# A transformer block with recurrent memory, forward and backward on one core: block-diagonal products in the backward loop and new priorities for its planner

## The chip, the cores and the metric

The kernel runs on one core of one Trainium2 chip. The metric is the device time of one execution in microseconds. The core has five engines with instruction queues of their own: PE (TensorE, matmuls; its weight loads are listed apart as PEld), DVE (VectorE), ACT (ScalarE), POOL (GpSimd) and SP (SyncE, which here only issues DMAs). SBUF is the memory on the chip in which engines read and write; PSUM takes the results of matmuls, here in eight banks.

## The reference

The output is the input x plus a memory-augmented attention of xn plus a squared-ReLU MLP of xn, where xn is the layer norm of x. All gradients (of x, the initial memory, four attention weights, two MLP weights and two biases) are outputs too. x has 2048 rows of 512; there are 32 heads of 128. What matters here is the attention, a recurrence over 64 segments:

```python
for s in range(n_seg):                       # 64 segments of 32 rows, M = 8
    xs = x[:, s * seg_len:(s + 1) * seg_len, :].copy()
    h = jnp.concatenate([mem, xs], axis=1)   # 8 memory rows, 32 tokens
    q = jnp.einsum('btd,dhe->bhte', h, Wq)
    k = jnp.einsum('btd,dhe->bhte', h, Wk)
    v = jnp.einsum('btd,dhe->bhte', h, Wv)
    scores = jnp.einsum('bhqe,bhke->bhqk', q, k) * scale
    scores = jnp.where(mask[None, None], scores, -1000000000.0)
    p = _softmax(scores, axis=-1)
    o = jnp.einsum('bhqk,bhke->bhqe', p, v)
    o = jnp.einsum('bhte,hed->btd', o, Wo)
    mem = o[:, :M, :].copy()                 # memory of the next segment
    outs.append(o[:, M:, :])
```

The backward pass walks the segments from the last to the first: the gradient of a segment's memory rows is an input of the segment before it, so the 64 segments form one chain.

## The kernel before, in words

The program has three stages: the forward pass, the backward loop over the segments, and the weight gradients as large products, which read back from memory (HBM) what the loop stored. Only the backward loop is changed.

In the loop the 32 heads lie as 8 groups (index i, NI = 8) of 4 (index j, JQ = 4); head (i, j) has its rows on the 32 partitions of quadrant j. Four segments make a block (SPB = 4, 16 blocks). The rows of a segment are split in two sets: the rows of the segment's chain ("A"), and the leading tokens ("L"), the first 8 tokens of each segment, 32 rows a block, which don't wait for the recurrence and are done for a whole block at once.

For each block `l_pre` does the leading tokens' part: it loads their V, K, Q and P, computes gL (the incoming gradient times Wo), dP (ps_dPL), the softmax's backward on DVE (btL, dSL), its transpose dSTLL, and dQ (ps_dqL, into dLN). `l_post` computes their gradients of x (ps_dRL) from what was stored. For each segment `load` fetches its operands and lets POOL spread some of them into block-diagonal tiles: BDP, BDL, BPK, BLK, BSLK, BDSL. `chain` is the recurrence itself:

- ps_gO: the segment's gradient rows times Wo; ps_gOT: their transposes, copied to SBUF as gOT by DVE or ACT
- ps_dP: from gOT and V; then `smax_bwd` on DVE, four steps on btA and brA, whose last writes dS into the tile named maskA
- after dS, on DVE: the copy of its memory columns to dSp, and two transposes, dSTA and dSTL, which lie in the tile named PB; POOL spreads dS's memory columns into BSK
- dV (part 2, `blocks`), dK (part 1, `mixed`) and dQ (part 0, `diag`): products into PSUM (ps_d), copied to dN by ACT or DVE, transposed to dT by DVE and multiplied by the weights (ps_dRA, 32 matmuls each, all three into one bank)
- ps_dL: the gradients of dK and dV for the leading tokens (`keys_part`)
- R_A: the sum, copied out of PSUM in two halves; ps_gm picks its memory rows, and DVE writes them over the memory rows of the gradient of the segment before (tile gT, a part of PA). With that copy (PA<-ps_gm) a segment ends, and the next one's ps_gO may begin.

`blk_out` transposes the block's gradient rows back (ps_gN), copies them to the tile gNat and stores them in S_GOA for the weight gradients.

A product of 32x32 pieces, one for each head, can be made in two ways. `diag` gives each head a matmul of 32 rows on 32 columns at its own place in the array, 16 for four groups. `blocks` needs the four heads of a group side by side in one tile with zeros elsewhere (block-diagonal) and makes one matmul of 128 on 128 for them.

The order of the instructions is not the order of the source. Each call of `plan.add` records an operation with its cost on each engine that may do it; `_Plan.run` then places them one by one. An operation's rank is the length of the work that hangs on it plus a number of its own from the table BIAS, and three numbers in PAR say how the rule weighs waiting. Each engine executes its queue in the order found.

## Time and profile before

| | |
|---|---|
| time, median of 3 runs | 2801.01 us (2796.82 to 2802.35) |
| span of the profiled execution, first to last instruction | 2798.3 us |
| busy in the span | PE 95%, PEld 55%, DVE 47%, ACT 35%, POOL 29% |
| granted TensorE clock, mean | 0.995 |
| instructions | 125071 |

The page gives the profiled execution as its span; no other time of it is listed. A page's busy PE includes what a pipelined matmul waits inside the array, so PE at 95% is not PE at its peak. Rows of the profile name a line, an engine, an operation and output<-inputs by tile; a line can be that of a helper that many operations share, so the tile names tell them apart. "issue" is time for which the profile names no wait.

### The profile page before, as it was taken

The page shows a single profiled execution, that of the slowest core. Times are in us where ns is not written, and L with a number is a line of the kernel's source. Part 1 is how long each engine was busy: PE and PEld are TensorE (multiplying, and loading weights), DVE is VectorE, ACT ScalarE, POOL GpSimd, SP SyncE. Part 2 cuts the span into 40 slices and gives each one's busy share as a digit, 9 for nine tenths or more (in the row PEclk, how much of TensorE's full clock was granted, in tenths as well). Part 3 has the DMA queues.
Part 4 walks back from the last instruction along what each step waited for, and adds up shares of the span by engine and source line. Part 5 has one row for each costly group of instructions (what it writes and reads, how often), then busy time and mean ns, then how long its engine had stood idle before and what let it go on. Part 6 is the DMA issues. An engine that isn't in the chain of part 4 may idle for free.

```text
span 2798.3 us, 125071 instructions
## 1 busy us (share of the span) xinstructions
PE 2664.6 (95%) x54888; PEld 1538.5 (55%) x55072; DVE 1327.3 (47%) x3327; ACT 985.8 (35%) x2012; POOL 824.8 (29%) x2431
## 2 busy tenths in 40 slices
PE   8998999999999999999999999999999899999999
PEld 6664555555555555575555555555555444444444
DVE  5544455555455555565455455555455402232322
ACT  4333444444444444364444444444444300000000
POOL 1111111111111111145555555555555301112210
PEclk9999999999999999999999999999999999999999
DMA  6657656555557566647777676777766698788861
GB/s 211 202 172 205 180 160 175 164 166 163 156 169 186 169 185 175 177 118 178 187 181 187 179 189 179 189 192 190 188 182 177 201 344 273 232 255 270 257 185 42
DMA packets 499792, 530.91 MB, mean 190 GB/s; under 512 B 223845, under 2 KB 325398, under 8 KB 497070
## 3 DMA queue, kind: packets, MB, share of 16 engines
q1 hardware_dynamic: 480254, 463.06, 59.9%
q0 software_dynamic: 15056, 53.56, 5.6%
q8 instruction: 430, 7.05, 1.1%
q10 hardware_dynamic: 3936, 6.29, 0.7%
q14 instruction: 116, 0.95, 0.1%
HBM read 249.77 MB, written 237.52 MB: 174 GB/s over the span
## 4 chain that ended last, share of the span: by engine, by line
PE 45%; DVE 4%; issue 3%; DMA 3%; ACT 1%; POOL 1%; SPq 0%; DVEq 0%; ACTq 0%; POOLq 0%
PE ps_gw L1690 14%; PE ps_dRA L1370 8%; PE ps_gw L1694 5%; PE ps_gO L538 3%; PE ps_dRL L1370 3%; PE ps_d L624 2%; DMA dLN<-S_GNL 2%; PE ps_d L573 1%; PE ps_d L599 1%; PE ps_gOT L429 1%; PE ps_d L588 1%; PE ps_gm L1524 1%; PE ps_gL L538 1%; PE ps_dL L1481 1%; PE ps_dP L1468 1%
## 5 line engine op out<-in xcount | busy, mean ns | idle before, releaser
L1370 PE MATMUL ps_dRA<-WA,dT 128*32 128x512 bf16 x6144 | 377.0, 381 | 5.3 <-issue 2.5
L1690 PE MATMUL ps_gw<-WA,WB 128*128 128x512 bf16 x1505 | 330.6, 379 | 1.6
L1690 PEld LDWEIGHTS <-WB 128*128 128x128 bf16 x1896 | 185.4, 98 | 225.0 <-issue 1.7
L538 PEld LDWEIGHTS <-PA 128*32 128x32 bf16 x8192 | 195.4, 96 | 192.3 <-DVE PA L1190 22.3
L435 ACT CAST dN<-ps_d 128x512 bf16<-128x512 f32 x372 | 207.4, 590 | 184.7 <-PE ps_d L599 112.3
L1370 PEld LDWEIGHTS <-dT 128*32 128x32 bf16 x6144 | 151.8, 96 | 154.2 <-DVE dT L517 17.3
L433 DVE CAST gwo<-ps_gw 128x512 bf16<-128x512 f32 x64 | 40.0, 685 | 399.9 <-PE ps_gw L1690 268.5
L435 ACT CAST gwo<-ps_gw 128x512 bf16<-128x512 f32 x64 | 33.1, 598 | 510.2 <-PE ps_gw L1690 357.3
L517 DVE STREAM_TRANSPOSE dT<-dN 128x256 f32<-128x256 f32 x384 | 165.4, 437 | 72.1 <-ACT dN L435 66.5
L1020 POOL TENSOR_TENSOR P<-P,rsA 128x320 bf16<-128x320 bf16 x64 | 46.2, 722 | 458.8 <-DVE rsA L1015 244.1
L624 PEld LDWEIGHTS <-PB 32*32 32x32 bf16 x8192 | 119.8, 92 | 76.4 <-DVE PB L1168 23.9
L1701 POOL DMA_DIRECT2D out_dram<-gwo x96 | 71.6, 753 | 293.9 <-ACT gwo L435 265.1
L538 PE MATMUL ps_q<-WA,PA 128*32 128x512 bf16 x2048 | 145.2, 382 | 5.5 <-DVE PA L1190 3.7
L1039 PE MATMUL ps_RA<-WB,OT 128*32 128x256 bf16 x4096 | 129.0, 277 | 17.7 <-DVE OT L517 13.6
L538 PE MATMUL ps_k<-WA,PA 128*32 128x512 bf16 x2048 | 144.9, 381 | 0.3 <-DVE PA L1190 0.3
L435 ACT CAST kN<-ps_k 128x512 bf16<-128x512 f32 x125 | 73.4, 587 | 194.1 <-PE ps_k L538 172.2
L538 PE MATMUL ps_v<-WA,PA 128*32 128x512 bf16 x2048 | 140.7, 379 | 0.0
L1039 PEld LDWEIGHTS <-OT 128*32 128x32 bf16 x4096 | 103.9, 98 | 46.2 <-DVE OT L517 32.0
L538 PE MATMUL ps_gO<-WB,PA 128*32 128x512 bf16 x2048 | 126.4, 380 | 1.0 <-DVE PA L1528 1.0
L611 POOL COPY BDL<-bPLL 32x64 bf16<-32x64 bf16 x256 | 60.4, 236 | 218.4 <-PE ps_d L573 210.4
L433 DVE CAST qN<-ps_q 128x512 bf16<-128x512 f32 x62 | 42.9, 692 | 171.5 <-PE ps_q L538 169.5
L1254 PE MATMUL ps_dw<-sx,anT 128*128 128x512 bf16 x339 | 108.2, 384 | 6.6 <-DMA sx<-S_XN 2.8
(315 smaller groups left out, 5300.8 us busy)
## 6 DMA issues: line engine op xcount, KB each, us to landing
S_GN<-dN SPq DMA_DIRECT2D x192, 256.0 KB
WA<-S_GN SPq DMA_DIRECT2D x150, 256.0 KB
S_Q<-qN SPq DMA_DIRECT2D x64, 256.0 KB
S_K<-kN SPq DMA_DIRECT2D x64, 256.0 KB
S_V<-vN SPq DMA_DIRECT2D x64, 256.0 KB
S_ON<-oN SPq DMA_DIRECT2D x64, 256.0 KB
bqN<-S_Q SPq DMA_DIRECT2D x64, 256.0 KB
bkN<-S_K SPq DMA_DIRECT2D x64, 256.0 KB
```

The lines of the kernel that those rows point to most:

```text
L433: nc.vector.tensor_copy(out, in_)
L435: nc.scalar.copy(out, in_)
L517: self.plan.add({"DVE": 0.445}, lambda e, half=half: nc.vector.transpose(words(dst, half).rearrange("p (i c r) -> p i c r", i=4, c=2), src ...
L538: nc.tensor.matmul(bk()[32 * j:32 * (j + 1), :], lhsT=win(dc), rhs=Wt(dc, c0), start=(dc == 0), stop=(dc == DC - 1), tile_position=(0, 32 ...
L611: f(q_(dst, j)[:, :, j, 0:c], q_(src_f(), j))
L624: nc.tensor.matmul(bk()[32 * j:32 * j + m, k * P:(k + 1) * P], lhsT=lf(j, i), rhs=rf(j, i), start=(k == 0 and x == 0), stop=(x == n - 1), ...
L1039: nc.tensor.matmul(bk()[32 * c:32 * (c + 1), :], lhsT=sg.rows(OTt, i, j), rhs=Wo[:, JQ * i + j, dh * DH:(dh + 1) * DH], start=(i == 0 and ...
L1254: nc.tensor.matmul(bks[x]()[:], lhsT=anT[x][:, c, :], rhs=sx[z][:], start=(c == 0), stop=(c == TC - 1))
L1370: nc.tensor.matmul(bk()[32 * j:32 * (j + 1), :], lhsT=sg.rows(XT, i, j), rhs=wtf(t, i, j), start=(first and i == 0), stop=(last and i == N ...
L1690: nc.tensor.matmul(bks[n](), lhsT=HNc[:, rc, dc * P:(dc + 1) * P], rhs=gns[y][:, hf * 512:(hf + 1) * 512], start=(y == 0), stop=(y == NRC ...
L1694: nc.tensor.matmul(bks[n](), lhsT=gns[y][:, k * P:(k + 1) * P], rhs=GOc[:, rc, :], start=(y == 0), stop=(y == NRC - 1))
L1701: nc.gpsimd.dma_start(outWs[t][dc * P:(dc + 1) * P, 4 * hf:4 * hf + 4, j, :], wt[:].rearrange("p (i e) -> p i e", i=4))
```

## The change

All that changes lies in the backward loop.

- dK's chain term: `mixed` can now take block-diagonal terms (`full=True`). dS is spread into a new tile BDS, and 8 matmuls of 128x128 take the place of 32 of 32x32. The two banks of this product have a kind of their own ("x") instead of sharing three with the others.
- The leading tokens' dQ: the two terms' transposed dS is copied into a new block-diagonal tile BDQ, half a block's groups and one term at a time, and 16 matmuls of 128x128 take the place of 64 small ones.
- The leading tokens' dP: V of the memory rows and V of the leading tokens lie in one tile (V3), so one matmul of 64 columns takes the place of two of 32.
- `blk_out`: only the memory rows are transposed and copied out of the chip's memory, 32 rows of 128 columns in four matmuls side by side; the other rows, which the loop doesn't change, go from the gradient's input to S_GOA directly. There are 8 DMAs a block instead of 4.
- PAR's third entry and the whole table BIAS_2 are new, and with them the order.

```diff
-PAR = ((0.3, 0.3, 0.0), (0.61, 7.94, 4.04), (0.09, 2.05, 17.32))
+PAR = ((0.3, 0.3, 0.0), (0.61, 7.94, 4.04), (0.1, 0.72, 43.97))
...
-        34.6, 126.2, 225, -84.9, 411.2, 93.4, -139.6, 40.8, -2.7, -1, 50.3, -26.5, 101.4, 73.6, 181.6, -48.1,
+        15.7, 24.2, 97.5, -336.6, -23, -15.5, -22.7, 0, 6.5, -136.5, -220.1, -237.4, -153.9, -142.5, -8.8,
...
-        def mixed(self, nm, pre, terms, rkeys, dst, prio, lift=0.0):
+        def mixed(self, nm, pre, terms, rkeys, dst, prio, lift=0.0, full=False, inter=False, kind=None):
 
-            bks = [self.bank("d", [P, 512], F32, "ps_" + nm) for _ in range(2)]
+            bks = [self.bank("x", [P, 512], F32, "ps_" + nm) for _ in range(2)]
...
                         for x, (lf, rf) in enumerate(terms):
+                            if full:
+                                nc.tensor.matmul(bk()[:, k * P:(k + 1) * P], lhsT=lf(i), rhs=rf(i),
+                                                 start=False, stop=(x == len(terms) - 1), skip_group_check=True)
+                                continue
                             for j in range(JQ):
...
-        VTL = [tl("VTL%d" % x, TR) for x in range(2)]
...
-        LT0, LT1 = (tl("LT%d" % x, TR) for x in range(2))
+        LT0, V3 = tl("LT0", TR), tl("V3", [P, 3, NI, JQ, RA])
+        VTL, LT1 = [V3[:, 1], V3[:, 0]], V3[:, 2]
+        V2 = [V3[:, 1:3], V3[:, 0:3:2]]
...
+        BDS = tl("BDS", TR)
...
+        BDQ = tl("BDQ", [P, NI // 2, JQ, RL])
+        nc.gpsimd.memset(BDQ[:], 0.0)
...
                 for i in range(NI):
-                    for c, VX in enumerate((VTL[p], VTM)):
-                        for j in range(JQ):
-                            nc.tensor.matmul(q_(bk(), j)[:, i, 32 * c:32 * c + 32], lhsT=LT0[:, i, j, :],
-                                             rhs=VX[:, i, j, :], start=(i == 0 and c == 0), stop=True,
-                                             tile_position=(0, 32 * j), skip_group_check=True)
-            A(pe(0.45, "w", 64), dp, both("LT0") + both("LT1") + [("VTL", p)], [bk, "btL"])
+                    for j in range(JQ):
+                        nc.tensor.matmul(q_(bk(), j)[:, i, :], lhsT=LT0[:, i, j, :], rhs=V2[p][:, :, i, j, :],
+                                         start=(i == 0), stop=True, tile_position=(0, 32 * j), skip_group_check=True)
+            A(pe(0.3, "w", 32), dp, both("LT0") + both("LT1") + [("VTL", p)], [bk, "btL"])
...
-            sg.diag("f", "dqL", [
-                (lambda j, i: q_(dSTLL, j)[:, i, 0, :], lambda j, i: q_(kLN[p], j)[:, i, :], 32),
-                (lambda j, i: q_(dSTLL, j)[:, i, 1, :], lambda j, i: q_(KM, j)[:, i, :], 32),
-            ], lambda h: ["dSTLL", K("kLN")] + both("LT1"), ("dLN", dLN), 1)
+            for h in range(2):
+                bq = sg.bank("f", [P, 512], F32, "ps_dqL")
+                for c, X in enumerate((kLN[p], KM)):
+                    for j in range(JQ):
+                        def cp(e, c=c, j=j, h=h):
+                            f = {"DVE": nc.vector.tensor_copy, "POOL": nc.gpsimd.tensor_copy}[e]
+                            f(q_(BDQ, j)[:, :, j, :], q_(dSTLL, j)[:, 4 * h:4 * h + 4, c, :])
+                        A({"DVE": 0.13, "POOL": 0.28}, cp, ["dSTLL"], [("BDQ", j)], 1)
+
+                    def mm(e, h=h, bq=bq, c=c, X=X):
+                        for k in range(4):
+                            nc.tensor.matmul(bq()[:, k * P:(k + 1) * P], lhsT=bd(BDQ, k), rhs=X[:, 4 * h + k, :],
+                                             start=(k == 0 and c == 0), stop=(c == 1), skip_group_check=True)
...
             sg.spread(BSK, "BSK", lambda: dS[:, :, 0:M], ["dS"], M, 0, {"POOL": 0.235})
+            sg.spread(BDS, "BDS", lambda: dS[:, :, M:KA], ["dS"], RA, 0, {"DVE": 0.17, "POOL": 0.41})
             part(1, lambda dst: sg.mixed(
                 "d1", [(lambda i: bd(BDSL, i), lambda i: qLN[p][:, i, :])],
-                [(lambda j, i: q_(dS, j)[:, i, M:KA], lambda j, i: q_(qN, j)[:, i, :])],
-                (lambda h: [K("qLN")] + bk4("BDSL"), lambda h: ["qN", "dS"]), dst, 0), False, False)
+                [(lambda i: bd(BDS, i), lambda i: qN[:, i, :])],
+                (lambda h: [K("qLN")] + bk4("BDSL"), lambda h: ["qN"] + bk4("BDS")), dst, 0, full=True), False, False)
...
-            bk = sg.bank("f", [P, D], BF16, "ps_gN")
+            A({"POOL": 0.3}, lambda e: nc.gpsimd.tensor_copy(
+                gNat[:, 0:P].rearrange("p (c v k) -> p c v k", c=DC, k=M), gT[p].rearrange("p c (v r) -> p c v r", r=RA)[:, :, :, 0:M]),
+              [("gT", p)] + [("gm", p, v) for v in range(SPB)], ["gNat"])
+            bk = sg.bank("f", [P, P], F32, "ps_gN")
...
-                    transpose_to(bk()[:, dc * P:(dc + 1) * P], gT[p][:, dc, :])
-            A(pe(0.222, "f", 4), tr, [("gT", p)] + [("gm", p, v) for v in range(SPB)], [bk, "gNat"])
-            sg.evict(lambda: gNat, bk, lambda: bk()[:], ["gNat"], 1, EV_B)
+                    nc.tensor.matmul(bk()[32 * dc:32 * (dc + 1), :], lhsT=gNat[:, 32 * dc:32 * (dc + 1)], rhs=ident[:],
+                                     start=True, stop=True, tile_position=(0, 32 * dc), skip_group_check=True)
...
+            for dc in range(DC):
+                sg.dma(lambda dc=dc: S_GOA[b * P:(b + 1) * P, dc * P:(dc + 1) * P].rearrange("(r v) d -> v r d", v=SPB)[:, 0:M],
+                       lambda dc=dc: gNat[32 * dc:32 * (dc + 1), P:2 * P], ["gNat2"], [])
             for v in range(SPB):
-                sg.dma(lambda v=v: S_GOA[b * P:(b + 1) * P, :].rearrange("(r v) d -> v r d", v=SPB)[v],
-                       lambda v=v: gNat[RA * v:RA * (v + 1)], ["gNat"], [])
+                sg.dma(lambda v=v: S_GOA[b * P:(b + 1) * P].rearrange("(r v) d -> v r d", v=SPB)[v, M:],
+                       lambda v=v: gflat[b * P + RA * v + M:b * P + RA * (v + 1)], [], [])
```

In the order that the planner finds, 254 of the 256 copies into BDS stand on DVE and 2 on POOL; of the 256 into BDQ 222 stand on DVE and 34 on POOL. Three places show what moves.

DVE, from dS to the transposes of dK and dQ, in the segment v = 2 of a block. The tile maskA is dS, PB holds its two transposes; dT_31380 and dT_31379 are those of dK and dQ before, dT_31378 that of dK after. Before:

```order
L1359 SCALAR_TENSOR_TENSOR maskA<-btA,bP_31372 128x320
L1500 COPY dSp_31345<-maskA 128x8x8
L1502 STREAM_TRANSPOSE PB<-dSp_31345 128x256
L1501 STREAM_TRANSPOSE PB<-maskA 128x256
L517 STREAM_TRANSPOSE dT_31380<-dN_31377 128x256 x2
L517 STREAM_TRANSPOSE dT_31379<-dN_31376 128x256 x2
```

After:

```order
L1376 SCALAR_TENSOR_TENSOR maskA<-btA,bP_31370 128x320
L624 COPY BDS<-maskA 32x8x32 x4
L1526 COPY dSp_31345<-maskA 128x8x8
L1527 STREAM_TRANSPOSE PB<-maskA 128x256
L1528 STREAM_TRANSPOSE PB<-dSp_31345 128x256
L518 STREAM_TRANSPOSE dT_31378<-dN_31375 128x256 x2
```

The four copies into BDS come first behind dS, and the copy and the transposes that dQ needs come behind them.

TensorE, from dP to dQ's product, in a segment that has the leading tokens' ps_dRL beside it; the first matmul of each group is shown. dT_31381 (before) and dT_31379 (after) belong to dV. The products with maskA or BDS are dK's chain term, with BDSL its leading term for the next segment, with PB dQ's. Before:

```order
L1468 MATMUL ps_dP<-bVT,gOT 32x40
...
L1370 MATMUL ps_dRL<-WA,LT_31360 32x512
...
L1370 MATMUL ps_dRA<-WA,dT_31381 32x512
...
L599 MATMUL ps_d_48441<-bqN,maskA 32x128
...
L1370 MATMUL ps_dRA<-WA,dT_31381 32x512
...
L624 MATMUL ps_d_49005<-bkN,PB 32x128
```

After:

```order
L1494 MATMUL ps_dP<-bVT,gOT 32x40
...
L1387 MATMUL ps_dRL<-WA,LT_31358 32x512
...
L1387 MATMUL ps_dRA<-WA,dT_31379 32x512
...
L607 MATMUL ps_d_46965<-bqN,BDS 128x128
...
L589 MATMUL ps_d_47427<-bqLN_31349,BDSL 128x128
...
L637 MATMUL ps_d_47433<-bkN,PB 32x128
```

Before, half of dV's 32 ps_dRA matmuls stand between dK's and dQ's products; after, all of them stand ahead of dK's, and only the four matmuls with BDSL stand between.

DVE, in the segment in which the leading tokens' softmax ends. Before:

```order
L1528 CAST PA<-ps_gm 128x4x8
L433 COPY LT_31360<-ps_gLT 128x512
L1354 TENSOR_TENSOR btL<-ps_dPL,bPLL_31357 128x512
L1356 TENSOR_REDUCE brL<-btL 128x8
L1357 TENSOR_TENSOR btL<-ps_dPL,brL 128x512
L517 STREAM_TRANSPOSE dT_31381<-dN_31378 128x256
L1359 SCALAR_TENSOR_TENSOR dSL_31359<-btL,bPLL_31357 128x512
```

After:

```order
L1555 CAST PA<-ps_gm 128x4x8
L1374 TENSOR_TENSOR btL<-ps_dPL,brL 128x512
L1376 SCALAR_TENSOR_TENSOR dSL_31357<-btL,bPLL_31355 128x512
L1425 STREAM_TRANSPOSE dSTLL<-dSL_31357 128x512
L1433 COPY BDQ<-dSTLL 32x4x32 x4
L434 COPY gOT<-ps_gOT 128x512
L1433 COPY BDQ<-dSTLL 32x4x32 x3
L434 COPY gOT<-ps_gOT 128x512
```

The softmax's first two steps moved into the segment before, and seven copies into BDQ stand ahead of the two gOT copies, for which ps_dP waits.

More of the change, by code (lines that the diff above doesn't have):

```diff
@@ L601, in mm @@
                                                  skip_group_check=True)
-                self.plan.add(pe(0.222 * len(terms), "d", 16 * len(terms)), mm, rkeys[1](half), [bk], prio)
+                cost = pe(0.22 * len(terms), "f", 4 * len(terms)) if full else pe(0.222 * len(terms), "d", 16 * len(terms))
+                self.plan.add(cost, mm, rkeys[1](half), [bk], prio)
                 self.evict(lambda half=half: dst[1][:, 4 * half:4 * half + 4, :].rearrange("p i e -> p (i e)"),
@@ L1331 @@
         BDP, BDL, BDSL = (tl(n, TR) for n in ("BDP", "BDL", "BDSL"))
-        for t_ in (BDP, BDL, BDSL):
+        BDS = tl("BDS", TR)
+        for t_ in (BDP, BDL, BDSL, BDS):
             nc.gpsimd.memset(t_[:], 0.0)
+        BDQ = tl("BDQ", [P, NI // 2, JQ, RL])
+        nc.gpsimd.memset(BDQ[:], 0.0)
         BPK, BLK, BSK, BSLK = (tl(n, [P, NI, JQ, M]) for n in ("BPK", "BLK", "BSK", "BSLK"))
```

45 lines of the change are left out of this document (28 added, 17 removed), and 27 rows, old and new, of the table BIAS_2.

## The prediction

> **What bounds the kernel now.** I read the page first, for the share of each engine, then the stretch of the backward loop alone, then the loop's own clock.
>
> ```profile
> span 2798.3 us, 125071 instructions
> PE 2664.6 (95%) x54888; PEld 1538.5 (55%) x55072; DVE 1327.3 (47%) x3327; ACT 985.8 (35%) x2012; POOL 824.8 (29%) x2431
> ...
> 1260.00:2209.00 949.00, 911.21 (x25763) 543.00 (x25755) 494.74 (x1232) 394.41 (x784) 527.49 (x1871) 1.00 0.72 184
> ...
> L1528 DVE CAST PA<-ps_gm x63: 191/192/193, 1259.8 to 2209.3; 128x32 bf16<-128x32 f32 x63
> ```
>
> The first two lines are the page's: the span, and the busy time of each engine. The third is one row of the table of busy time by stretch (PE, PEld, DVE, ACT, POOL, granted clock, DMA share, GB/s): in the loop TensorE shows 911 of 949 us at a granted clock of 1.00, DVE 495, POOL 527. The last comes from the view of one tile: the copy that closes a segment runs 63 times between 1259.8 and 2209.3 us, so 62 segments take 949.5 us, 15.3 us each, and 64 take about 980. Outside the loop and its two ends the change adds only two fills with zeros, so the forward stage and the weight products (from 2257 us on) keep their time.
>
> The chain of waits in the middle of the loop is almost all TensorE, and it prices the pieces:
>
> ```profile
> 1712.60 0.98 PE ps_dRA L1370 x16
> 1713.58 1.00 PE ps_d L624 x64
> ...
> 1722.16 0.45 PE ps_d L573 x8
> ...
> 1723.73 0.31 PE ps_dP L1468 x30
> ...
> 1726.89 0.56 PE ps_d L599 x32
> ...
> 1728.85 0.86 PE ps_dRA L1370 x16
> ...
> 1734.71 0.33 PE ps_gLT L429 x4
> ...
> 1736.51 0.56 PE ps_dPL L1404 x64
> ...
> 1750.30 0.55 PE ps_dqL L624 x32
> ...
> 1753.47 0.72 PE ps_dqL L624 x32
> ```
>
> Each row is a start, a length in us and the matmuls in it. Eight full 128x128 matmuls take 0.45 us, 56 ns each; the 32 small ones of dK's chain term (L599) take 0.56 us. A group of 16 dRA matmuls counts 0.86 us, but 0.98 us where the next group has another tile shape (the row ahead of L624): a change of shape costs about 0.12 us.
>
> How much of the loop is TensorE's own limit, and how much the chain through the other engines, shows in one segment of the timeline:
>
> ```profile
> 1769.31 0.27 PE L1468 MATMUL ps_dP<-bVT,gOT 128*32 128x40 bf16 x16
> ...
> 1769.69 0.49 DVE L1354 TENSOR_TENSOR btA<-ps_dP,bP 128x320 f32<-128x320 f32 x1 [0.27 <-PE ps_dP L1468]
> ...
> 1771.34 0.49 DVE L1359 SCALAR_TENSOR_TENSOR maskA<-btA,bP 128x320 bf16<-128x320 f32 x1
> ...
> 1771.96 0.50 POOL L611 COPY BSK<-maskA 32x64 bf16<-32x64 bf16 x2 [0.49 <-DVE maskA L1359]
> ...
> 1772.11 0.14 DVE L1500 COPY dSp<-maskA 128x64 bf16<-128x64 bf16 x1
> ...
> 1772.52 0.41 DVE L1502 STREAM_TRANSPOSE PB<-dSp 128x256 bf16<-128x256 bf16 x1
> ...
> 1773.72 0.23 PE L624 MATMUL ps_d<-bkN,PB 32*32 32x128 bf16 x4
> ```
>
> The second half of dP starts at 1769.31, dS (the tile maskA) is done at 1771.83, its two transposes at 1772.93, and dQ's product (L624) starts at 1773.72, because TensorE was busy until then: there are 0.79 us of slack. So in such a segment TensorE is the bound, and what is taken from it counts in full, until DVE's path from dP to dQ becomes longer by 0.79 us or TensorE's cover shorter by as much.
>
> **The change part by part: what TensorE saves.** dK's chain term goes from 32 matmuls in 0.56 us to 8 full ones in 0.45: 0.11 us, times 64 segments, 7.0 us. The full ones have the shape of the product with BDSL that now follows them, so one change of shape of 0.12 us goes too: 7.7 us. The leading tokens' dQ (L624 on ps_dqL) took 0.55 + 0.72 = 1.27 us a block; 16 full ones at 56 ns are 0.90: 0.37 us, times 16 blocks, 5.9 us. Their dP drops from 64 matmuls in 0.56 us to 32 of 64 columns; 30 of 40 columns take 0.31, so I take 0.31: 0.25 times 16, 4.0 us (between zero, should the wider ones cost twice as much, and that). In the block gradients' copy four transposes, which like those of ps_gLT are 0.33 us between other shapes, become four side by side in the array; I take 0.13 for them, from a quarter of 0.33 up to no gain: 0.2 times 16, 3.2 us. Together 27.8 us, if TensorE is the bound everywhere.
>
> **What the order makes of it.** The rows of the order stand in the part on the change. On DVE, four BDS copies now stand between dS and everything that waits for it: dK's product, and behind them the two transposes and dQ's product. On TensorE all of dV's dRA now stands ahead of dK's product and none of it between dK's and dQ's, so the filler has moved to where the four copies need it. In the block's first steps seven BDQ copies stand ahead of the two gOT copies.
>
> **What the copies cost.** The trace has no such copy on DVE; the nearest is the one from dS to dSp, with 64 elements a partition for BDS's 256. The rows are of the views of a tile, of the timeline and of the groups by shape (busy us, mean ns | idle before):
>
> ```profile
> L1500 DVE COPY dSp<-maskA x48: 133/146/292, 1267.2 to 2220.1; 128x64 bf16<-128x64 bf16 x48
> ...
> 1742.62 1.08 DVE L1500 COPY PB<-maskA 128x64 bf16<-128x64 bf16 x1
> 1742.62 1.03 POOL L1438 COPY bVT<-VR 128x1024 bf16<-128x1024 bf16 x1
> ...
> 1744.09 0.10 PEld L624 LDWEIGHTS <-PB 32*32 32x32 bf16 x4 [1.00 <-DVE PB L1501]
> ...
> L611 POOL COPY BDP<-bP 32x256 bf16<-32x256 bf16 x239 | 100.4, 420 | 8.6
> ...
> L611 POOL COPY BSK<-maskA 32x64 bf16<-32x64 bf16 x244 | 56.5, 232 | 34.2 <-DVE maskA L1359 24.1
> ```
>
> Its median is 146 ns, its longest 292, and once it took 1.08 us, just as long as the copy that POOL ran beside it, while TensorE waited 1.00 us. From dP to the first softmax step are 0.38 us (1769.31 to 1769.69), to dS done 2.52, the copies 4c, then 1.10 (1771.83 to 1772.93): dQ can start at 3.62 + 4c. TensorE's cover in a segment with four groups of 16 is 4 x 0.86 + 0.12 + 0.45 + 0.22 (half of eight full ones) = 4.23 us. So c up to 0.15 costs nothing, and c at its median just fits. With one copy of the four held up as in the longest of the row, 4c is 0.73 and TensorE waits 0.12 us, 8 us in 64 segments; with all four it is 1.17, the wait 0.56, and the sum 36 us. I take 8, since half of the dSp copies took 146 ns or less, close to the shortest. The lower end is zero. The far upper end is POOL's copy of BDS's own shape (BDP, 0.42 us): 4c = 1.68, a wait of 1.07 us, 68 us; I take DVE's row, since DVE makes these copies.
>
> The second new wait is on DVE in the block's first steps, where the leading tokens' softmax ends while TensorE computes gO. The two gOT copies are queued behind seven of BDQ, and dP, so the whole chain, waits for gOT. At 146 ns the seven are 1.0 us; part of it passes while TensorE still computes gO, gOT and d2. I take 0.5 us a block, 8 us; the ends are zero and 1.4 us a block (the seven at 0.2, nothing hidden), 22 us. Nothing is taken for POOL's small copy in `blk_out`, on which only a store waits, nor for the four further DMAs a block: they are issues of the SP queue of some 0.4 us, and the rows from memory to memory wait for nothing. What is queued behind them are the next loads, and TensorE waited for a late one (DVE's LT, from dLN) once in this loop:
>
> ```profile
> PE ps_dRL L1370 <- DVE LT L517: 2.2, 1, 2.2
> ```
>
> The sum: -27.8 + 8 + 8 = -11.8 us, so 2786.5 us of span. The medians are 2.7 us above that span, so 2789 us as a median.
>
> **The rivals.** *TensorE stays the bound everywhere.* DVE is only half busy in the loop, and the copies fit as c = 0.15 allows. Then the 27.8 us come in full: 2773. Against it: the segment with the BDQ copies has less cover than the one worked out.
>
> *DVE and POOL get in each other's way: slower.* The row at 1742.62 shows a DVE copy that lasts as long as POOL's. POOL starts its own copies of dS (BSK) at the moment at which the four BDS copies start, at 1771.96 here, and is busy 56% of the loop. If each of the four lasts as long as the longest dSp copy (0.292 us, its median and something over half of one BSK copy's 232 ns), the wait is the 0.56 us a segment worked out above, 36 us, with 8 for BDQ: -28 + 36 + 8 = +16, 2817 us; with BDQ at its end, 2831. It decides from the point at which more than two of the four copies are held up, since two (4c = 0.88) make 0.27 us a segment, 17 us, and with BDQ's 8 cancel what TensorE saves. For it speaks that POOL has copies of its own in hand at that moment in every segment; against it that the dSp copy, at the same place, has its median close to its shortest.
>
> The Trainium skill, "SBUF — State Buffer", section "Who interferes with whom", speaks against this change: a DVE copy in a two-port mode and GpSimd share a port pair under an exclusive lock, and the second to come blocks for the whole instruction. The trace agrees at 1742.62, 1.08 us beside 1.03. By that rule, with POOL never idle there, every copy waits and the slower rival holds.
>
> *Saving and waits cancel*, at two copies held up of four: within 0.2% of 2801, 2795.4 to 2806.6, about what a measurement of this kernel can tell from no change.
>
> **How the numbers follow.** Forecast 0.38 (2781 to 2795), TensorE bound everywhere 0.15, cancelled 0.13, slower 0.34. Faster 0.53, same 0.13, slower 0.34. The two lowest cases hold 0.53 and reach from 2768 (the 27.8 and some 5 us of rarer stalls, such as the longest gap before dL, below) to 2795; the slower case is cut at 2820, 11 us short of its end.
>
> ```profile
> PE ps_dL L1481 <- issue: 5.3, 4, 2.5
> ```
>
> The range, 2768 to 2820, has both signs; the forecast's own range is 2781 to 2795.
>
> **What would show it.** Right: dK's term at 0.45 us, dqL near 0.9 a block, segments near 15.1 us, BDS copies at a median under 0.18 us, and little wait of TensorE on BDS and PB. Wrong: BDS copies of 0.25 us and more beside POOL's copies, TensorE's waits on BDS, PB or gOT up by over 30 us in the loop, segments above 15.4 us. If segments shrink to 14.9, the cover was larger than I counted.

## The result and the profile after: slower by 4.4%

The changed kernel takes 2926.41 us (median of 4 runs, 2921.97 to 2930.72), the kernel before beside it 2800.53 (2796.82 to 2802.35): a ratio of 1.0442, 95% interval 1.0417 to 1.0466. The forecast was 2789, its range 2768 to 2820. The profiled run took 2927.07 us.

The page:

```profile
span 2925.3 us, 120206 instructions
PE 2672.5 (91%) x52072; PEld 1544.6 (53%) x52256; DVE 1508.9 (52%) x3802; ACT 989.3 (34%) x2013; POOL 844.0 (29%) x2485
```

The table of busy time by stretch for the loop (PE, PEld, DVE, ACT, POOL, granted clock, DMA share, GB/s):

```profile
1261.00:2337.00 1076.00, 921.74 (x23156) 552.06 (x23148) 677.38 (x1707) 398.36 (x787) 544.06 (x1921) 0.97 0.61 163
```

The copy that closes a segment, in the view of its tile (ns min/median/max, first and last start):

```profile
L1555 DVE CAST PA<-ps_gm x63: 180/192/193, 1260.9 to 2337.5; 128x32 bf16<-128x32 f32 x63
```

The 62 segments between the first and the last closing copy take 1076.6 us instead of 949.5, 17.4 each instead of 15.3. That is the whole difference: ahead of the loop and behind it nothing moved. TensorE is idle 154 us of the loop, against 38 before, VectorE has 183 us more work, and the granted clock fell from 1.00 to 0.97. TensorE's busy time in the loop did not fall, 921.7 us for 911.2, although it has fewer matmuls: a part of them ran at half clock (see the last section). By the starts of the closing copies, the first four segments (a block) take 87.2 us (60.3 before) and the other 14 full blocks 68.4 in the mean (61.3).

What TensorE waits for from 1340 to 2340 us (engine, line, waited for: us, times, longest):

```profile
PE ps_d L607 <- DVE BDS L624: 97.5, 57, 2.0
PE ps_gO L539 <- DVE PA L1555: 11.3, 16, 0.8
```

The groups by shape (busy us, mean ns | idle before):

```profile
L624 DVE COPY BDS<-maskA 32x256 bf16<-32x256 bf16 x254 | 134.7, 530 | 4.7
L1464 POOL COPY bVT<-VR 128x1024 bf16<-128x1024 bf16 x64 | 73.3, 1146 | 3.6 <-DMA VR<-S_V 0.7
```

The BDS copies take 530 ns in the mean, not 146, and TensorE stands idle for them in nearly every segment. The timeline of one segment shows why:

```profile
1336.26 0.27 PE L1494 MATMUL ps_dP<-bVT,gOT 128*32 128x40 bf16 x16
...
1338.49 0.49 DVE L1376 SCALAR_TENSOR_TENSOR maskA<-btA,bP 128x320 bf16<-128x320 f32 x1
1338.52 1.04 PE L1387 MATMUL ps_dRA<-WA,dT 128*32 128x512 bf16 x16
1338.63 1.25 POOL L1464 COPY bVT<-VR 128x1024 bf16<-128x1024 bf16 x1
...
1339.02 2.16 DVE L624 COPY BDS<-maskA 32x256 bf16<-32x256 bf16 x4
1339.94 0.52 POOL L624 COPY BSK<-maskA 32x64 bf16<-32x64 bf16 x2
1340.41 0.39 POOL L1467 COPY bVT<-V 128x256 bf16<-128x256 bf16 x1
...
1341.23 0.62 PE L607 MATMUL ps_d<-bqN,BDS 128*128 128x128 bf16 x8 [1.68 <-DVE BDS L624]
```

The first row is the second half of dP. GpSimd started its copy of V into bVT (bVT<-VR) 0.35 us before dS was done. The four BDS copies take 2.16 us beside it and GpSimd's next ones, TensorE's last filler (L1387) ends at 1339.56, and it waits 1.68 us.

The loop's start has a wait of its own. SyncE's queue there, in the timeline:

```profile
1235.02 9.37 SPq L480 DMA_DIRECT2D S_GOA<-in_grad_out_dram  x10
...
1255.65 8.30 SPq L480 DMA_DIRECT2D S_GOA<-in_grad_out_dram  x11
1264.57 8.16 SPq L480 DMA_DIRECT2D S_GOA<-in_grad_out_dram  x9
1273.38 0.38 SPq L480 DMA_DIRECT2D bqN<-S_Q  x1
```

What TensorE waits for from 1255 to 1330 us:

```profile
PE ps_d L607 <- DMA bqN<-S_Q: 16.5, 2, 9.4
```

The row copies' issues in the view of their tile:

```profile
L480 SPq DMA_DIRECT2D S_GOA<-in_grad_out_dram x64: 702/712/1828, 1235.0 to 1302.3; - x64
```

All 64 row copies are issued between 1235 and 1302 us, 0.71 us each, and the first block's loads stand behind them: qN is issued at 1273.38, and TensorE waits 9.4 us for one load.

### The profile page after: what moved, and what is told of

Read it like the earlier page. It is cut to its first block, busy times and chain, and to the rows that moved or that the text cites. A ratio compares the mean times of both kernels' runs of the same rounds, so it can differ in the third digit from the quotient of the medians.

```text
span 2925.3 us, 120206 instructions
## 1 busy us (share of the span) xinstructions
PE 2672.5 (91%) x52072; PEld 1544.6 (53%) x52256; DVE 1508.9 (52%) x3802; ACT 989.3 (34%) x2013; POOL 844.0 (29%) x2485
## 4 chain that ended last, share of the span: by engine, by line
PE 39%; DVE 12%; issue 3%; DMA 3%; SPq 1%; ACT 1%; POOL 0%; DVEq 0%; ACTq 0%; POOLq 0%
PE ps_gw L1724 14%; PE ps_dRA L1387 6%; PE ps_gw L1728 5%; DVE BDS L624 4%; PE ps_gO L539 3%; PE ps_d L637 3%; PE ps_d L574 2%; PE ps_d L607 1%; PE ps_dRL L1387 1%; SPq L480 1%; DVE maskA L1376 1%; PE ps_gOT L430 1%; DVE dT L518 1%; DVE btA L1371 1%; DVE brA L1373 1%
## 5 line engine op out<-in xcount | busy, mean ns | idle before, releaser
L1387 PE MATMUL ps_dRA<-WA,dT 128*32 128x512 bf16 x6144 | 374.0, 387 | 5.5 <-DVE dT L518 5.4
L436 ACT CAST dN<-ps_d 128x512 bf16<-128x512 f32 x383 | 213.7, 588 | 264.1 <-PE ps_d L607 204.1
L1387 PEld LDWEIGHTS <-dT 128*32 128x32 bf16 x6144 | 154.0, 98 | 175.9 <-DVE dT L518 22.3
L637 PEld LDWEIGHTS <-PB 32*32 32x32 bf16 x8192 | 133.1, 98 | 57.7 <-DVE PB L1181 24.1
L607 PE MATMUL ps_d<-bqN,BDS 128*128 128x128 bf16 x512 | 45.3, 230 | 119.7 <-DVE BDS L624 99.4
L624 POOL COPY BSLK<-dSL 32x64 bf16<-32x64 bf16 x256 | 59.2, 231 | 276.4 <-PE ps_dL L1507 267.7
L624 DVE COPY BDS<-maskA 32x256 bf16<-32x256 bf16 x254 | 134.7, 530 | 4.7
L624 POOL COPY BDP<-bP 32x256 bf16<-32x256 bf16 x256 | 101.4, 396 | 115.7 <-PE ps_d L574 104.7
```

Source lines behind the costliest of these rows:

```text
L436: nc.scalar.copy(out, in_)
L607: nc.tensor.matmul(bk()[:, k * P:(k + 1) * P], lhsT=lf(i), rhs=rf(i), start=False, stop=(x == len(terms) - 1), skip_group_check=True)
L624: f(q_(dst, j)[:, :, j, 0:c], q_(src_f(), j))
L637: nc.tensor.matmul(bk()[32 * j:32 * j + m, k * P:(k + 1) * P], lhsT=lf(j, i), rhs=rf(j, i), start=(k == 0 and x == 0), stop=(x == n - 1), ...
L1387: nc.tensor.matmul(bk()[32 * j:32 * (j + 1), :], lhsT=sg.rows(XT, i, j), rhs=wtf(t, i, j), start=(first and i == 0), stop=(last and i == N ...
```

## The experiments

Two theories stand against each other at first: that the copies (BDS, BDQ, rows) hold up the chain, and that the new priorities do. Every kernel was timed beside the kernel before on its own chip, so ratios are compared; a point is 1% of before, 28 us. "First" and "others" are blocks of four segments, in us, from the starts of the closing copies of the profiled run.

| run | what | ratio (95% interval) | first | others |
|---|---|---|---|---|
| | the change | 1.0442 (1.0417 to 1.0466) | 87.2 | 68.4 |
| e1 | rows wait for the block's end | 1.0506 (1.0480 to 1.0532) | 68.5 | 70.5 |
| e2 | BDS copies left out | 1.0175 (1.0150 to 1.0200) | 82.8 | 63.2 |
| e3 | BDS made as sums | 1.0321 (1.0293 to 1.0349) | 86.0 | 65.7 |
| e4 | GpSimd's spreads left out | 1.0271 (1.0244 to 1.0298) | 82.6 | 64.9 |
| e5 | 16 row copies | 1.0415 (1.0379 to 1.0452) | 68.3 | 68.5 |
| e6 | e5 without BDS, BDQ | 1.0128 (1.0086 to 1.0169) | 64.8 | 63.0 |
| e7 | before + BDS | 1.0214 (1.0171 to 1.0258) | 65.1 | 65.1 |
| e8 | before + copying back | 1.0310 (1.0274 to 1.0346) | 81.8 | 65.3 |
| e9 | e5, old priorities | 1.0338 (1.0319 to 1.0357) | 70.0 | 67.2 |
| e10 | e7, BDS copies left out | 1.0055 (1.0036 to 1.0074) | 59.0 | 62.6 |
| e11 | BDQ copies left out | 1.0330 (1.0312 to 1.0348) | 86.0 | 66.3 |
| e12 | before + dP in one product | 0.9981 (0.9969 to 0.9993) | 60.6 | 60.8 |
| e13 | before + new priorities | 1.0260 (1.0224 to 1.0296) | 63.2 | 65.3 |
| e14 | before + BDQ | 1.0744 (1.0712 to 1.0776) | 74.2 | 74.7 |
| e15 | e8 with 16 row copies | 1.0212 (1.0180 to 1.0243) | 59.0 | 65.0 |
| e16 | e3 and e5 together | 1.0276 (1.0245 to 1.0306) | 66.7 | 66.1 |
| e17 | e5, bVT in quarters | 1.0308 (1.0272 to 1.0343) | 66.7 | 66.7 |

### What the BDS copies cost

Runs e2, e3 and e4 keep the order and touch the copies alone: left out; made as sums; GpSimd's spreads left out.

```diff
                 def cp(e, j=j):
+                    if dk == "BDS":                                                # e2
+                        return
+                    if dk in ("BDP", "BDL", "BPK", "BLK", "BSK", "BSLK", "BDSL"):  # e4
+                        return
...
+                    if dk == "BDS" and e == "DVE":                                 # e3
...
+                            nc.vector.tensor_reduce(q_(dst, j)[:, :, j, 0:c], q_(src_f(), j).unsqueeze(3), axis=AX.X, op=ALU.add)
```

> The changed kernel with the 256 BDS copies planned in their places but not issued (so the chain term of dK is multiplied with a matrix that was never filled, and TensorE no longer waits for dS through it). Theory that the copies hold the chain dS, dK, dQ (their 134.7 us on VectorE, 99 us of it seen as idle time of TensorE ahead of the dK products): 80 to 130 us less, 2796 to 2846 us, steady segments 15.0 to 15.6 us. Rival (the new priorities and the late rows are what costs, VectorE's copies only happen to be waited for last): less than 50 us gained, above 2876 us.

> The changed kernel with the same 254 BDS copies made on VectorE by a sum over an axis of one element instead of a copy, same places and same data. Theory that the copies are held up by GpSimd's (mean 530 ns, median 283, up to 1598): a sum is not held, all come to 0.3 to 0.45 us with no tail, and 20 to 60 us come back, 2866 to 2906 us. Rival (the copies cost by their own length and by the longer dependence from dS to dK): their mean rises above 530 ns or the tail stays, and the time is 2920 to 2950 us.

> The changed kernel with all copies of the spreading helper on GpSimd (those that fill BDP, BDL, BPK, BLK, BSK, BSLK and BDSL) planned but not issued; the two BDS copies that the plan gives to GpSimd stay. Those block-diagonal matrices are never filled. Theory that GpSimd holds VectorE's copies: the BDS copies fall to 0.21 to 0.25 us each with hardly any tail, and 60 to 110 us come back, 2816 to 2866 us. Rival (own length and dependence): BDS stays above 0.4 us in the mean and less than 20 us come back. A gain with BDS still slow would say that TensorE waited for GpSimd's own products.

Without the copies the ratio falls by 2.7 points, about 75 us: the copies do hold the chain (the time of 2843.73 us is within what their theory gave; the 75 us are a little under its 80, the 15.8 us a segment a little above its 15.6). The view of the tile in e3, then in e4 (ns min/median/max):

```profile
L626 DVE TENSOR_REDUCE BDS<-maskA x254: 406/409/417, 1242.9 to 2307.4; 32x256 bf16<-32x256 bf16 x127
```

```profile
L626 DVE COPY BDS<-maskA x254: 214/217/1448, 1245.0 to 2292.1; 32x256 bf16<-32x256 bf16 x127
```

As sums they last 0.41 us whatever GpSimd does, nearly twice the copy's bare 0.217, and yet 1.2 points come back: a good part of the loss is not their length but their being held up. With hardly a copy of GpSimd's beside them the median is 217 ns and 1.7 points come back (2871.36 us, just above the theory's 2866). But length counts too, since both are slower than e2. In e4 TensorE waits 16.3 us for the unhindered copies in 48 segments (1340 to 2140 us), 0.34 us each; in the changed kernel it waits 78.8 us in 46. The 0.96 points between e4 and e2 are not the price of these copies alone: e4 leaves out GpSimd's spreads as well, and TensorE waits 19.4 us for BDQ there against 4.4 in e2.

Sorted by the GpSimd copy with which each overlapped longest (worked out from the starts and ends in the trace of the changed kernel):

| beside | BDS copies | mean ns | max ns |
|---|---|---|---|
| bVT<-VR (1.04 us alone) | 71 | 969 | 1598 |
| bVT<-V (0.39) | 46 | 610 | 618 |
| BSK (0.23) | 103 | 277 | 300 |
| the other copies of a spread | 33 | 275 | 417 |
| nothing | 1 | 216 | 216 |

Run e17 is e5 with a shorter neighbour and nothing else:

```diff
-                VT[:, :, :, M:KA]..., VR[:]...
+            [nc.gpsimd.tensor_copy(VT[:, 2 * x:2 * x + 2, :, M:KA]..., VR[:, 2 * x:2 * x + 2]...) for x in range(4)]
```

> The changed kernel with one row copy a block (the run of ratio 1.0415) and one more edit: GpSimd's copy of V into bVT (1.04 us, beside which BDS copies took 0.95 us and up to 1.6) is made in four instructions of a quarter each, at the same place; every other engine keeps its order word for word and all results are whole. Theory that a VectorE copy waits for the end of the one GpSimd instruction that it meets: BDS beside bVT falls from 1080 ns in the mean to 0.3 to 0.55, the mean of all from 533 to 300 to 400, and 20 to 35 us come back, ratio 1.029 to 1.035, although GpSimd's four pieces together take longer. Rival (VectorE stays shut out while GpSimd has a run of copies, whatever their length): BDS beside bVT stays above 0.9 us and the ratio at 1.038 to 1.045.

```profile
1316.51 1.66 POOL L1464 COPY bVT<-VR 128x256 bf16<-128x256 bf16 x4
1316.92 1.33 DVE L624 COPY BDS<-maskA 32x256 bf16<-32x256 bf16 x4
```

```profile
L624 DVE COPY BDS<-maskA 32x256 bf16<-32x256 bf16 x254 | 104.3, 411 | 4.7
```

These are e17's timeline and its groups by shape. Four BDS copies now take 1.33 us beside bVT, their mean is 411 ns (533 in e5, a little above the 300 to 400 expected), and 1.07 points come back although GpSimd's copy takes 1.66 us in all here. In most cases the hold ends with one GpSimd instruction; the exception is told at the end.

### What the order costs

Run e7 puts dK's product alone into the kernel before, under its own priorities; e10 is the same order without the copies; e9 has all four products under the old priorities; e13 has the new priorities and no other part of the change.

```diff
+            at, bias, plan.bias = plan.at, plan.bias, ()   # e7, e9, e10: the added operations have a bias of zero
+            sg.spread(BDS, "BDS", lambda: dS[:, :, M:KA], ["dS"], RA, 0, {"DVE": 0.17, "POOL": 0.41})
+            plan.at, plan.bias = at, bias
...
-PAR = (..., (0.09, 2.05, 17.32))
+PAR = (..., (0.1, 0.72, 43.97))            # e13: PAR and BIAS_2 of the changed kernel
...
+            plan.at += JQ                  # e13: the entries of added operations are skipped
```

> The kernel before, with its own priorities, and dK's chain term alone as a block-diagonal product (the BDS copies, with a bias of zero, and 64 x 8 full matmuls). Theory that the four copies ahead of dS's transposes cost in any order: blocks of 63.5 to 67 us, ratio 1.012 to 1.035. Rival (it is the new priorities that leave no cover): ratio 0.995 to 1.005.

> All four rebuilt products, with the one row copy a block of the run with 16, but under the priorities of the kernel before (PAR and BIAS_2 as they were, the added operations with a bias of zero). It stands beside the run that differs from it in the priorities alone (ratio 1.0415, BDS copies 533 ns in the mean, half of their time beside GpSimd's bVT copies). Theory that the new priorities put the dS copies beside GpSimd's longest copies: BDS mean 0.22 to 0.27 us, no copy above 0.5, ratio 1.010 to 1.030. Rival (any order has them held up): BDS mean above 0.4 us, ratio 1.035 to 1.05.

> The kernel before with dK's block-diagonal product, in the very order of the run with ratio 1.0214, but the BDS copies not issued (the matrix stays unfilled). It splits those 2.1%: theory that the copies cost even where none is held up (4 x 0.234 us ahead of dS's transposes): 30 to 60 us come back, ratio 0.995 to 1.010. Rival (the planner's order, disturbed by four more operations, is what costs, by its wait of the weight products on dT and the other stalls): less than 20 us come back, ratio above 1.014.

> The kernel before with every product as it was (no BDS, no BDQ, the old copying back) and only the new priorities (PAR and BIAS_2 of the changed kernel, the entries of the added operations skipped). Theory that the new order loses by itself, because it puts GpSimd's long copies beside dS and the leading tokens' store and reload late: blocks of 62.5 to 65.5 us, ratio 1.015 to 1.035, PB's transposes or dSp held up beside bVT. Rival (the order is harmless and only the copies in it cost): ratio 0.995 to 1.008.

The BDS copies of e7, in the view of the tile:

```profile
L623 DVE COPY BDS<-maskA x247: 171/224/443, 1269.9 to 2281.9; 32x256 bf16<-32x256 bf16 x124
```

Under the old priorities GpSimd makes BSK beside dS, and no BDS copy lasts over 0.443 us. They cost all the same: e7 is at 1.0214, e10 at 1.0055, so 1.6 points, 44 us. In e9 the BDS mean is 247 ns (three copies met bVT<-V, up to 614, above the 0.5 us expected), which otherwise is what the theory of the priorities gave; the time, 1.0338, fell between the two forecasts. Between e9 and e5 lie 0.8 of e5's 4.2 points; they differ in the priorities, and in dP's planned cost, which e9 leaves as it was.

On the old products they make 2.6 points, 73 us, as their theory said. The copy of dS's memory columns and the step that writes dS, in e13 by shape; before they stood at 185 and 504 ns in the mean:

```profile
L1360 DVE SCALAR_TENSOR_TENSOR maskA<-btA,bP 128x320 bf16<-128x320 f32 x64 | 40.7, 636 | 6.1
...
L1512 DVE COPY dSp<-maskA 128x64 bf16<-128x64 bf16 x48 | 21.2, 443 | 1.1
```

Of the 48 dSp copies, 21 lie beside bVT<-VR and take 727 ns in the mean; before, none lay there, and that copy of GpSimd's ran mostly beside the softmax steps on btA, which take 491 ns with it and without it. So the new table moves GpSimd's longest copy from work that it doesn't disturb to dS, where it does, with BDS or without. That explains only a part of the 73 us, how much was not settled. TensorE's two longest waits in e13 from 1340 to 2140 us are on a transpose of the leading tokens (LT) and on dS:

```profile
PE ps_dRL L1371 <- DVE LT L518: 12.5, 9, 4.0
PE ps_d L600 <- DVE maskA L1360: 11.7, 12, 3.9
```

Before, neither LT nor dS kept it waiting over 2 us in all in that stretch; the late reload of the leading tokens, the other half of the theory, has its share as well.

### The leading tokens' copies and dP

Run e11 leaves the BDQ copies out of the changed kernel; e14 puts BDQ alone into the kernel before, with the code of the change; e12 puts dP's one product there, its planned cost unchanged.

```diff
                         def cp(e, c=c, j=j, h=h):
+                            return                                        # e11
...
-                    for c, VX in enumerate((VTL[p], VTM)):                # e12
...
+                        nc.tensor.matmul(q_(bk(), j)[:, i, :], lhsT=LT0[:, i, j, :], rhs=V2[p][:, :, i, j, :], ...)
             A(pe(0.45, "w", 64), dp, both("LT0") + both("LT1") + [("VTL", p)], [bk, "btL"])
```

> The changed kernel with the BDQ copies planned but not issued (the leading tokens' dQ is multiplied with an unfilled matrix). The prediction's own term for them: 8 us, between 0 and 22, so 2904 to 2926 us at the before of that comparison, a ratio of 1.036 to 1.044. Rival (copies on VectorE delay the gOT copies and, through them, every later wait): 30 us or more, ratio under 1.034.

> The kernel before, under its own priorities, with the leading tokens' dQ alone as a block-diagonal product (16 BDQ copies a block). The prediction's terms: 5.9 us saved on TensorE and 8 us of waits, a ratio of 0.999 to 1.003. Rival (16 more copies a block on VectorE hold up the chain's own copies in any order, as the 31 us in the changed kernel suggest): ratio 1.006 to 1.015.

> The kernel before with the leading tokens' dP alone in one product (32 matmuls of 64 columns for 64 of 32) and its planned cost left as it was, so that every engine keeps its order word for word. The prediction's term: 4.0 us less, a ratio of 0.9986, and ps_dPL at 0.31 us in place of 0.56. Rival (64 columns take twice as long as 32, so nothing is saved): ratio 1.000, ps_dPL at 0.5 us or more. A difference of 4 us is near what the comparison can tell; the product's own row decides.

BDQ costs 1.1 points, 31 us, the rival's side of e11. In the changed kernel's trace 108 of its 222 copies on VectorE have a gOT copy as the next step of the chain behind them, 61 a transpose dT, 45 the writing of dS or a BDS copy. In e14 neither forecast was near: +7.4%. TensorE's waits there, from 1340 to 2140 us:

```profile
PE ps_d L599 <- DVE maskA L1361: 36.6, 26, 2.8
PE ps_dqL L1427 <- DVE BDQ L1421: 18.8, 14, 2.6
PE ps_dRL L1372 <- DVE LT L517: 16.1, 9, 3.9
PE ps_dP L1483 <- DVE gOT L433: 11.5, 6, 4.5
```

They name dS, BDQ, LT and gOT, all made by VectorE; which of the planner's moves is behind the rest of the 205 us was not settled.

The one part that gains is dP: 0.9981. The view of the tile in the kernel before, then in e12:

```profile
L1404 PE MATMUL ps_dPL<-VTL,LT x512: 176/179/190, 1243.4 to 2165.6; 128*32 128x32 bf16 x171
L1404 PE MATMUL ps_dPL<-LT,LT x512: 176/178/190, 1243.5 to 2165.7; 128*32 128x32 bf16 x171
```

```profile
L1404 PE MATMUL ps_dPL<-V,LT x512: 192/193/203, 1244.1 to 2160.1; 128*32 128x64 bf16 x171
```

One matmul of twice the columns lasts 14 ns longer, and half of the matmuls are gone. In the chain of waits of e12 the product takes 0.30 us (at 1730.78), as its theory said, where it took 0.56 before. This version is 5 us faster than the kernel before (0.07 to 0.31% by the interval), and so the fastest of all that were run.

### The copying back

Run e8 puts the changed `blk_out` alone into the kernel before, e15 does so with one row copy a block; e1 and e5 change the row copies of the changed kernel.

```diff
-                       lambda v=v: gflat[...], [], [])
+                       lambda v=v: gflat[...], ["gNat2"], [])                               # e1
...
-            for v in range(SPB): ...
+            sg.dma(lambda: S_GOA[...].rearrange(...)[:, M:], lambda: gflat[...].rearrange("(v r) d -> v r d", v=SPB)[:, M:],
+                   [("gm", p, 1)], [])                                                      # e5, e6, e9, e15 to e17
```

> Only edit to the changed kernel: the 64 further memory-to-memory row copies are again made to wait for the block before (as the 64 others are), so that the planner cannot issue them all ahead of the first block's loads. Theory of the flood at the start (the first block took 87 us for its four segments against 60 before): 25 to 30 us come back, 2896 to 2902 us, and the first four segments fall to 60 to 66 us, the later blocks stay at 68 us. Rival (the loads catch up anyway, the late start is hidden behind the constants' loads): 2918 to 2927 us.

> The changed kernel with the further row copies made by one DMA a block (16 instead of 64), which waits for the end of the block's third segment from the end of the chain, so that neither the first block's loads nor a block's last stands behind a queue of them. Theory of the flood (64 issues ahead of the first loads cost the first block 19 to 27 us; late ones block the loads behind them): first block 64 to 70 us, other blocks 67.5 to 68.5, 15 to 25 us less than the changed kernel, a ratio to before of 1.035 to 1.039. Rival (the first block is slow from the new order of its loads, whatever the row copies do): first block above 78 us, ratio 1.042 to 1.046.

> The kernel before, with its own priorities, and only the copying back of the block gradients changed as in the changed kernel (memory rows transposed side by side, 64 further row copies that wait for nothing). Theory of the flood: first block 72 to 86 us against 60.3, the other blocks as before (60 to 62), ratio 1.004 to 1.010. Rival (the flood came from the new priorities of the loads): first block 59 to 63 us, ratio 0.997 to 1.001.

> The kernel before with the changed copying back and one row copy a block, which waits for the block's third segment from the end: the run of ratio 1.031 without its flood of 64. Theory that the flood was one part (the first block's 21 us) and a steady cost of SP's issues the other: first block 60 to 64 us, the others 63 to 66 as there, ratio 1.018 to 1.026. Rival (the 64 issues ahead put SP behind for the whole loop): blocks of 60.5 to 62.5, ratio 0.998 to 1.008.

The flood is shown in both orders: the first block is 87.2 us (the change) and 81.8 (e8) with it, 68.3 (e5) and 59.0 (e15) without. But e8's 1.0310 lies far above both of its forecasts, because its other blocks are slow too, 65.3 us against 61.3. And e1 lost more later than it gained there, against both forecasts. Its waits from 1340 to 2140 us:

```profile
PE ps_d L607 <- DMA bqN<-S_Q: 24.3, 9, 3.8
```

Eight S_GOA issues at each block's end now stand ahead of the load of qN, for which TensorE hardly waited in that stretch of the changed kernel. One row copy a block (e5) keeps the first block at 68.3 and the others at 68.5; by the blocks that is 19 us, by the ratios 0.3 points with overlapping intervals, which alone would not show it. Under the old priorities the change of the copying back costs 2.1 points even without the flood (e15, as its theory said): the planner's order came out otherwise, and what in it costs was not settled.

### What is left

Run e6 is e5 with the edits of e2 and e11, run e16 is e5 with that of e3.

> The same 16 row copies, and neither the BDS nor the BDQ copies issued (both block-diagonal matrices stay unfilled; places in the order kept). What is left is the new order with TensorE's smaller products. Theory that the copies and the flood are all that costs: TensorE's 28 us come through, blocks of 59 to 60.5 us, ratio 0.988 to 0.996. Rival (the new priorities cost by themselves): blocks of 61.5 to 63 us, ratio 1.002 to 1.012.

> The changed kernel with two things mended: the BDS copies made by a sum over one element (410 ns each, held up by nobody) and one row copy a block. All results are whole. Theory that the two are separate: the 1.1 points of the one and the 0.3 of the other add up, ratio 1.027 to 1.031, first block near 66 us, the others near 65. Rival (the row copies are hidden once the segments are shorter, or the other way round): ratio 1.031 to 1.034.

With BDS, BDQ and the flood gone the changed kernel is still 1.3% above before: the rival held, its end of 1.012 passed by a little. TensorE's longest wait in e6 from 1340 to 2140 us:

```profile
PE ps_dRA L1389 <- DVE dT L518: 37.5, 13, 5.0
```

The chain of waits in one of its blocks:

```profile
1699.69 6.57 DMA dLN<-S_GNL
...
1706.29 0.04 DVE LT L518
...
1706.65 0.41 DVE dT L518
...
1707.11 3.44 PE ps_dRA L1389 x32
```

A transpose of the leading tokens (LT), for which VectorE waits on a load, stands ahead of the chain's own dT, and TensorE waits up to 5 us for that. This wait on dT is 1.6 us in the changed kernel from 1340 to 2140 us and 27.7 in e2: it comes out when the waits on BDS go. So the parts don't add: left out one by one, BDS, BDQ and the flood bring 2.7, 1.1 and 0.3 points, together only 3.1. An order that moves this transpose was not tried. In e16 the two mends add up as far as intervals of 0.3 points can tell (1.21 and 0.27 points apart, 1.66 together).

## Why the prediction was wrong, step by step

- **The cost of a copy.** This is the step that failed first. c was taken from the dSp row, 146 ns, with one of four held up, 8 us in all; its far end was 68. Alone a BDS copy takes 217 ns, beside BSK 277, beside bVT<-VR 969 in the mean; all in all they cost 75 us, above the far end. The row at 1742.62, 1.08 us beside 1.03, was the right price for a copy that meets bVT<-VR, and was counted as one event.
- **Who stands beside it.** The order was read on VectorE and TensorE, and GpSimd was taken to start BSK beside dS, as before. GpSimd's own order had moved too: bVT stands there now. The rival named the mechanism, but capped a copy at 0.292 us and itself at 2831, and the range left the rest out.
- **The path and its cover.** The wait was worked out for dQ's product, with dK's product counted as cover (0.45 of the 4.23 us, and 0.22 for the product with BDSL behind it). But dK's product reads BDS and waits for the copies itself: that is where the 97.5 us fell, on L607. In the segment at 1338 TensorE has work from the second half of dP (1336.26) until 1339.56, 3.30 us; dS takes 2.72 of them, so 0.58 us are left for the four copies, which at 217 ns need 0.87 and took 2.16. Even copies that nobody holds make TensorE wait 0.34 us a segment (e4).
- **The priorities had no term.** They were read only as the place of each added copy. Alone they cost 73 us.
- **The clock had no term.** By the trace's clock records the loop ran 72 us at half clock, before 3. An estimate of what that cost is half of it at most, some 36 us, part of which is in the sums above: e2, without the copies, still has 31 us at half clock.
- **BDQ:** 31 us for 8, above the end of 22. Half of them do stand ahead of gOT, as foreseen; that others stand ahead of dT, dS and BDS was not.
- **"Wait for nothing"** was read as harmless. It is what lets the planner issue 64 of them ahead of the first loads, at 0.71 us each, not 0.4 (the trace of before has such copies, S_GOL from in_grad_out, with a median of 0.65): the first block of the change takes 27 us more, 19 of them come back in e5.
- **Right:** dP's saving (4.0 said, 5.3 measured by e12's ratio), and the sign by which the change would show itself wrong: BDS above 0.25 us, waits on it above 30 us, segments above 15.4. Whether the other savings of TensorE came in can't be told, since e6, which has them all, is slower for the order.

The Trainium skill, "SBUF — State Buffer", section "Who interferes with whom", had it right: a copy of VectorE's in a two-port mode is shut out by GpSimd for the whole instruction, a reduce never is. The trace agrees: beside bVT<-VR the copy took 969 ns in the mean, the sum in e3 never over 417. It doesn't agree that the hold is one instruction long each time (below). The same section says that an operation with two inputs in SBUF contends with GpSimd's reads, and that one with a single input there, outside the two-port modes, doesn't. The trace agrees: dS's step (btA and bP, both in SBUF) took 719 ns in the mean beside bVT<-VR in e13, while the steps that write btA from PSUM and at most one tile in SBUF stayed at 491 beside it in the kernel before. The prediction cited the rule and gave its own estimate more weight.

## What to carry to other kernels

Price a VectorE copy by what GpSimd does at that place in the new order, and read GpSimd's order as closely as the bound engine's. A table of priorities belongs to the program it was made for, as these runs suggest: any part of this change under the old table cost 2 to 7%, except the one that left the order alone, and the new table alone cost 2.6%. It is not shown that the order was to blame each time: e7 lost mostly by its copies, and e14 and e15 were not settled. A transfer without a dependence is not free, because a greedy planner puts it ahead of everything that has one.

## What the runs showed of the hardware

The hold doesn't always end with one GpSimd instruction. In e17, 15 of the 254 copies took 2.0 us: each began 0.04 us behind the start of a BSK copy and ended only when five more GpSimd copies had passed, the four pieces of bVT<-VR and bVT<-V, though elsewhere in this run a BDS copy got in after each piece. In the changed kernel 15 copies took 1.6 us in the same way, through bVT<-VR and bVT<-V. Why these and not the others was not tried.

The granted clock is lower where TensorE waits more. From 1600 to 2000 us, before, after and e14 (the columns of the table by stretch):

```profile
1600.00:2000.00 400.00, 387.39 (x11015) 231.01 (x11016) 212.22 (x522) 169.63 (x337) 224.89 (x796) 1.00 0.72 186
```

```profile
1600.00:2000.00 400.00, 347.60 (x8819) 207.38 (x8812) 253.41 (x633) 150.58 (x298) 203.41 (x719) 0.98 0.64 167
```

```profile
1600.00:2000.00 400.00, 350.79 (x8982) 205.37 (x8983) 199.39 (x527) 139.14 (x277) 189.04 (x677) 0.94 0.59 159
```

With TensorE busy 97% it is 1.00, but at 87 and 88% 0.98 and 0.94: the busy share alone doesn't set it. The clock records show only 1 and 0.5, so these are means over stretches at full and at half clock. In the changed kernel's loop 16 of TensorE's 18 waits of over 2.0 us have a stretch of half clock, 3.4 us long or a multiple of it, that begins before the wait ends or within a microsecond of its end; of the 44 waits of 1.5 to 1.9 us none has. One such wait, of 2.04 us from 1390.0, comes in the segment with the 1.6 us copies, and from 1392.7 to 1395.9 the granted clock is 0.50. Inside such a stretch 16 matmuls of ps_dRA take 1.71 us, outside 0.86, so one stretch costs TensorE up to 1.7 us (an estimate, half of 3.4) on top of the wait. Two us is no rule, though: in e17 only 6 of 16 such waits have one, and in e16 3 of 57 waits of 1.0 to 1.5 us do. What decides it was not tried.
